# Twenty more small memsets in GpSimd's program, ahead of the constants for the attention sums

## Chip, cores, metric

One core of one Trainium2 chip. The metric is the time of one execution in microseconds (us) on the device; medians of several executions are quoted, and verdicts need 2% to call a kernel faster or slower. A run can fall in a slow state, with a lower granted TensorE clock; such runs are left out of ratios.

## The reference

A layer norm of x (2048 x 512), a sliding, dilated local attention on it (32 heads of 16, a window of 8 keys 2 apart), a gated MLP on it (512 to 1792 to 512), and their combination:

```python
    xn = _layernorm(x, axis=-1)
    s = _A_ref(xn, A_wqkv, A_wo)
    g = _silu(_B_ref(xn, B_w_gate, B_w_up, B_w_down))
    return x + s * g
```

## The kernel before

The kernel works on four groups of 512 positions. GpSimd has little to do: a few constants, and the power -1/2 for the norm of the later tiles. In the code and the views, xn is a normalized tile of x, pk the products of queries and keys, h the gated products of the MLP, pv the products of weights and values; dsum and hsum are constant tiles of zeros and ones by which TensorE sums pk into the attention logits (L_ps) and pv into the outputs (o_ps). The parts that matter here (cuts marked):

```python
    hsum = const.tile([P, H], BF16, name="hsum")
    dsum = const.tile([P, NC, H], BF16, name="dsum")

    def sum_constants():

        nc.gpsimd.memset(dsum[:], 0.0)
        for c in range(NC):
            nc.gpsimd.memset(dsum[:, c, 8 * c : 8 * c + 8], 1.0)
            band(dsum[:, c, 8 * c : 8 * c + 8], 0, 16, 16, 1, 8)   # two affine selects
        for j in range(WL):
            nc.gpsimd.tensor_copy(...)                              # hsum, from ident
    # ...
    def moments(t):
        # ... bn_stats, bn_aggr and + EPS on VectorE
        nc.gpsimd.tensor_tensor(out=rstd[:, t, :], in0=rstd[:, t, :], in1=mhalf[:], op=ALU.pow)
    # ...
    def logits(j):
        # ... TensorE: L_ps, with lhsT=dsum[:, c, :], rhs=the products pk of VectorE
    # ... in the main program, for the first group:
    for t in range(TPQ, 2 * TPQ):
        moments(t)
    sum_constants()
    # ... projections; VectorE: normalize, then pk and h in turn; TensorE: g_ps, u_ps, then logits
```

The softmax here doesn't subtract the row's maximum and nothing guards it: scores larger than these inputs give would overflow.

## Time and profile before

| | |
|---|---|
| time, median of 6 in all | 229.99 us (229.64 to 230.21) |
| span of the profiled execution, first to last instruction | 228.0 us |
| busy share of TensorE / VectorE / ScalarE / GpSimd | 98% / 65% / 57% / 6% |
| GpSimd's constants finished | 21.38 us |
| next GpSimd work, released by VectorE | 32.98 us |
| first read of dsum by TensorE | about 34.05 us |

The first four rows say who limits, the last three where the change goes in: a gap of 11.6 us in a spare engine, with two users behind it. The lines are in the prediction.

### The profile page before, as it was taken

To read this page: it belongs to the slowest core of one execution; us is meant where nothing else is said; L and a number is where in the kernel's file an instruction comes from. 1 tells how busy PE (TensorE), PEld (TensorE's weight loads), DVE (VectorE), ACT (ScalarE), POOL (GpSimd) and SP (SyncE) were. 2 spreads that over 40 slices of the span, in tenths; PEclk is the share of its full clock that TensorE was granted. 3 is DMA by queue.
4 is the path that set the end of the run, shared out by engine and by line. 5 is a ranking of instruction groups with operands and counts; after the bars stand their busy time and mean duration, and the time that the engine had idled before them with its cause. 6 is when DMAs were issued, how large, how long until landed. Compare 5 with 4: busy or idle time off the path is not lost.

```text
span 228.0 us, 3495 instructions
## 1 busy us (share of the span) xinstructions
PE 222.4 (98%) x1300; PEld 106.8 (47%) x1320; DVE 147.6 (65%) x234; ACT 129.8 (57%) x213; POOL 12.8 (6%) x44
## 2 busy tenths in 40 slices
PE   8999999999999999999999999999999999999993
PEld 6864444444444444444444444444444444444453
DVE  4585996999496298865945369735476429943324
ACT  3779769774423876467621686746642387647210
POOL 1046023100000000110000000000000000000000
PEclk9999999999999999999999999999999999999999
DMA  6999589971399211110287511110149700001011
GB/s 166 354 372 372 146 169 197 247 202 38 101 195 206 70 25 29 26 29 0 92 169 168 139 30 23 26 35 5 39 119 206 169 27 3 0 6 26 0 45 48
DMA packets 31264, 24.62 MB, mean 108 GB/s; under 512 B 10896, under 2 KB 31248, under 8 KB 31248
## 3 DMA queue, kind: packets, MB, share of 16 engines
q1 hardware_dynamic: 31248, 24.41, 42.8%
q8 instruction: 10, 0.16, 0.3%
q14 instruction: 6, 0.05, 0.1%
HBM read 18.74 MB, written 4.34 MB: 101 GB/s over the span
## 4 chain that ended last, share of the span: by engine, by line
PE 95%; ACT 2%; issue 1%; DVE 0%; ACTq 0%; DVEq 0%
PE u_ps L238 21%; PE y_ps L394 21%; PE g_ps L238 19%; PE qkv_ps L238 17%; PE s_ps L410 6%; PE L_ps L295 3%; PE o_ps L357 3%; PE warm_ps L220 2%; PE q_ps L238 1%; ACT u L384 1%; ACT L382 1%; PE tr L203 1%; PE den_ps L315 0%; ACT xnT L212 0%; ACT ge L382 0%
## 5 line engine op out<-in xcount | busy, mean ns | idle before, releaser
L238 PE MATMUL u_ps<-xnT,wu_sb 128*128 128x512 bf16 x224 | 57.5, 379 | 0.3
L238 PE MATMUL g_ps<-xnT,wg_sb 128*128 128x512 bf16 x213 | 56.3, 379 | 0.4
L394 PE MATMUL y_ps<-wd_sb,h 128*128 128x512 bf16 (+1 forms) x236 | 50.2, 366 | 0.1
L386 DVE TENSOR_TENSOR h<-ge,u 128x512 bf16<-128x512 bf16 x56 | 23.7, 424 | 37.0 <-ACT u L384 36.6
L284 DVE TENSOR_TENSOR pk<-q_sb,k_sb 128x2048 bf16<-128x2048 bf16 x32 | 37.5, 1216 | 7.0 <-ACT k_sb L259 7.0
L382 ACT ACTIVATE ge<-g_ps 128x512 bf16<-128x512 f32 x56 | 33.5, 598 | 14.9 <-PE g_ps L238 13.8
L384 ACT ACTIVATE u<-u_ps 128x512 bf16<-128x512 f32 x56 | 33.5, 598 | 14.7 <-PE u_ps L238 14.7
L238 PE MATMUL qkv_ps<-xnT,wqkv_sb 128*128 128x512 bf16 (+1 forms) x203 | 40.5, 354 | 0.3
L343 DVE TENSOR_TENSOR pv<-E,v_arr 128x2048 bf16<-128x2048 bf16 x32 | 38.6, 1218 | 0.2 <-issue 0.2
L394 PEld LDWEIGHTS <-h 128*128 128x128 bf16 x238 | 23.3, 98 | 25.3
L238 PEld LDWEIGHTS <-wu_sb 128*128 128x128 bf16 x224 | 21.9, 98 | 26.6 <-issue 0.3
L238 PEld LDWEIGHTS <-wg_sb 128*128 128x128 bf16 x224 | 21.3, 98 | 27.3 <-issue 3.0
L402 ACT ACTIVATE sl<-y_ps 128x512 bf16<-128x512 f32 (+1 forms) x17 | 9.7, 572 | 41.4 <-PE y_ps L394 39.0
L238 PEld LDWEIGHTS <-wqkv_sb 128*128 128x128 bf16 x224 | 21.8, 98 | 19.8 <-issue 0.4
L418 DVE TENSOR_TENSOR m<-s_ps,sl 128x512 bf16<-128x512 f32 (+1 forms) x17 | 11.2, 657 | 22.2 <-PE s_ps L410 22.2
L410 PE MATMUL s_ps<-wo_sb,oT 128*128 128x512 bf16 (+1 forms) x66 | 15.8, 366 | 0.2
L262 ACT ACTIVATE vst<-qkv_ps 128x512 bf16<-128x512 f32 x16 | 9.6, 598 | 6.5 <-PE qkv_ps L238 6.5
L188 POOL TENSOR_TENSOR rstd<-rstd,mhalf 128x1 f32<-128x1 f32 x12 | 7.7, 640 | 87.4 <-DVE rstd L185 87.4
L259 ACT ACTIVATE k_sb<-qkv_ps 128x512 bf16<-128x512 f32 (+1 forms) x20 | 10.2, 516 | 3.5 <-PE qkv_ps L238 3.2
L369 DVE TENSOR_TENSOR oT<-o_ps,rb 128x1024 bf16<-128x1024 f32 x8 | 9.4, 1216 | 3.1 <-DMA rb<-rs_d 3.1
L256 ACT ACTIVATE q_sb<-qkv_ps 128x512 bf16<-128x512 f32 (+1 forms) x16 | 8.7, 544 | 3.2 <-PE qkv_ps L238 3.0
L410 PEld LDWEIGHTS <-oT 128*128 128x128 bf16 x68 | 6.7, 98 | 7.2
(46 smaller groups left out, 105.9 us busy)
## 6 DMA issues: line engine op xcount, KB each, us to landing
v_arr<-vT SPq DMA_DIRECT2D x16, 520.0 KB, 5.4
vT<-vst SPq DMA_DIRECT2D x16, 128.0 KB, 1.8
out_dram<-o_t SPq DMA_DIRECT2D x15, 128.0 KB, 1.8
wg_sb<-in_B_w_gate_dram SPq DMA_DIRECT2D x2, 896.0 KB, 10.7
wu_sb<-in_B_w_up_dram SPq DMA_DIRECT2D x2, 896.0 KB, 12.3
wd_sb<-in_B_w_down_dram SPq DMA_DIRECT2D x1, 1792.0 KB, 12.3
wqkv_sb<-in_A_wqkv_dram SPq DMA_DIRECT2D x3, 512.0 KB, 5.2
x_sb<-in_A_x_dram SPq DMA_DIRECT2D x3, 512.0 KB, 11.6
```

The lines of the kernel that those rows point to most:

```text
L238: nc.tensor.matmul(ps, lhsT=w[:, dk, lo : lo + P], rhs=xnT[j][:, dk, i0 : i0 + n], start=(dk == 0), stop=(dk == NC - 1),)
L259: nc.scalar.activation(out=k_sb[:, c, lo : lo + n], in_=ps, func=AF.Copy)
L262: nc.scalar.activation(out=vst[:], in_=ps, func=AF.Copy)
L284: nc.vector.tensor_tensor(out=pk[:], in0=st[j]["q"][:], in1=k_sb[:, :, off : off + TQ], op=ALU.mult)
L343: nc.vector.tensor_tensor(out=pv[:], in0=st[j]["E"][:, wh, :].unsqueeze(1).to_broadcast([P, 4, TQ]), in1=st[j]["va"][:, 4 * g : 4 * g + 4, ...
L382: nc.scalar.activation(out=ge[:], in_=g_ps[:], func=AF.Gelu_apprx_tanh)
L384: nc.scalar.activation(out=u[:], in_=u_ps[:], func=AF.Copy)
L386: nc.vector.tensor_tensor(out=h[:], in0=ge[:], in1=u[:], op=ALU.mult)
L394: nc.tensor.matmul(y[:], lhsT=st[j][fc][:, tt * P : (tt + 1) * P], rhs=wd_sb[:, fc, cols], start=(fc == 0), stop=(fc == NF - 1),)
L402: nc.scalar.activation(out=sl[:], in_=y[:], func=AF.Silu)
L410: nc.tensor.matmul(s[:], lhsT=st[j]["oT"][:, g, tt * P : (tt + 1) * P], rhs=wo_sb[:, g, cols], start=(g == 0), stop=(g == NC - 1),)
L418: nc.vector.tensor_tensor(out=m[:], in0=s[:], in1=sl[:], op=ALU.mult)
```

## The change

No gain is intended by the memsets themselves: they write a tile that nobody reads, and so ask what work costs that is added to an engine with time to spare.

```diff
+    filler = const.tile([P, 1], F32, name="filler")
+
     def sum_constants():
 
+        for _ in range(20):
+            nc.gpsimd.memset(filler[:], 0.0)
+
         nc.gpsimd.memset(dsum[:], 0.0)
```

## The prediction

> **What bounds the kernel now.** I read four views of the profile, from the whole to the place that the change touches: the page (busy shares and the chain that ended last), the list of who waited for whom, GpSimd's timeline from 16 to 22 us, and the timelines of TensorE and VectorE around the first use of what GpSimd makes there. On the page:
>
> ```profile
> PE 222.4 (98%) x1300; PEld 106.8 (47%) x1320; DVE 147.6 (65%) x234; ACT 129.8 (57%) x213; POOL 12.8 (6%) x44
> ...
> PEclk9999999999999999999999999999999999999999
> ...
> PE 95%; ACT 2%; issue 1%; DVE 0%; ACTq 0%; DVEq 0%
> ```
>
> TensorE is busy for 222.4 of 228.0 us at a full granted clock, and 95% of the chain that ended last runs over TensorE's own instructions. POOL (GpSimd) is busy for 6% and does not appear in that chain at all. So a microsecond of GpSimd's time counts only if TensorE comes to wait for it, directly or through VectorE or ScalarE. The list of waits says how often anybody waits for GpSimd today, and how long GpSimd itself sits idle:
>
> ```profile
> POOL rstd L188 <- DVE rstd L185: 87.4, 12, 52.0
> ...
> DVE xn L194 <- POOL rstd L188: 0.9, 2, 0.4
> ```
>
> Each line gives us in total, how often, and the longest. The first says that GpSimd idled 87.4 us in total before its twelve small power operations. The second is the only line in which another engine waits for GpSimd: 0.9 us in two pieces, on VectorE. The third view is where the new instructions go, between the power at 16.35 us and the memset of dsum at 16.95 us:
>
> ```profile
> 16.35 0.65 POOL L188 TENSOR_TENSOR rstd<-rstd,mhalf 128x1 f32<-128x1 f32 x1 [0.46 <-DVE rstd L185]
> 16.95 0.20 POOL L145 MEMSET dsum<- 128x128 bf16 x1
> 17.21 0.13 POOL L147 MEMSET dsum<- 128x8 bf16 x1
> 17.41 0.25 POOL L130 TENSOR_SCALAR_AFFINE_SELECT dsum<-dsum 128x8 bf16<-128x8 bf16 x1
> 17.73 1.07 POOL L134 TENSOR_SCALAR_AFFINE_SELECT dsum<-dsum 128x8 bf16<-128x8 bf16 x1
> 18.74 0.10 POOL L147 MEMSET dsum<- 128x8 bf16 x1
> 18.91 0.19 POOL L130 TENSOR_SCALAR_AFFINE_SELECT dsum<-dsum 128x8 bf16<-128x8 bf16 x1
> ...
> 20.45 0.93 POOL L150 COPY hsum<-ident 32x32 bf16<-32x32 bf16 x4
> ...
> 32.98 1.39 POOL L188 TENSOR_TENSOR rstd<-rstd,mhalf 128x1 f32<-128x1 f32 x1 [11.60 <-DVE rstd L185]
> ```
>
> The columns are start and duration in us. GpSimd finishes its constants at 20.45 + 0.93 = 21.38 us and then does nothing until 32.98 us: 11.60 us of idle time, ended by VectorE and not by itself. The fourth view shows who uses the constants first:
>
> ```profile
> 33.09 1.03 PE L238 MATMUL u_ps<-xnT,wu_sb 128*128 128x512 bf16 x4
> 34.05 1.91 PE L295 MATMUL L_ps<-pk,dsum 128*32 128x512 bf16 x32
> ```
>
> dsum is first read by TensorE at about 34.05 us (its weight load), 13.5 us after its last affine select ended (20.31 + 0.19 = 20.50 us). hsum is first read at 51.5 us (the view of the tile hsum: first weight load of line 315), 30 us after its copies ended.
>
> **What the Trainium skill says.** GPSIMD Engine Reference, section 2.1 "Instruction dispatch", describes that completion gates whatever waits on an instruction's semaphore, while the next Pool instruction without such a wait may start before it. This matters, because the program of the changed kernel shows 19 of the 20 memsets waiting on GpSimd's own semaphore: they write the same tile, so each waits for the one before. The trace agrees that such a wait costs. Four unrelated memsets in a row at the start begin at 0.31, 0.34, 0.37 and 0.41 us, so about 0.03 us apart, though each is shown with 0.10 us. Where an affine select waits for the memset ahead of it, it begins 0.17 us after it (18.74 to 18.91).
> SBUF — State Buffer, section "Who interferes with whom": a VectorE instruction with two SBUF inputs contends with a GpSimd instruction that reads SBUF, not with one that only writes it, and a VectorE instruction in a two-port mode contends with GpSimd either way; the one that comes second blocks in full. The trace agrees for the first: the affine select at 17.73 took 1.07 us instead of 0.19, and it lies beside VectorE's product pk from 17.53 to 18.74 us. The new memsets only write. Whether the normalizations beside them (xn, line 194) are in a two-port mode, no view here settles.
> Perfetto Trace Analysis, section "GPSIMD Engine Instruction": time GpSimd instructions by the distance from start to start, not by their shown duration. I do so below.
>
> **The change, part by part.** Nothing is removed. The order of instructions on all other engines is the same as before, line numbers apart, and no other engine waits for the new tile. Its one column per partition might shift later tiles' addresses; nothing in the profile gives that a cost, and I book none.
> Added are 20 memsets of 128x1 f32. The distance of a waiting instruction behind a short memset is 0.17 us (three cases: 18.74 to 18.91, and the same for the columns that start at 19.31 and 19.88). The first starts at about 16.95 us, in the place of the dsum memset. 19 x 0.17 = 3.23 us to the start of the last, and the dsum memset follows without a wait, some 0.1 us later: about 3.3 us in all. If the waits were free, 20 x 0.03 = 0.6 us; if each cost what the affine selects do from start to start (18.91 to 19.18, 0.27 us), 5.4 us. So 3.3 us, 0.6 to 5.4.
> Moved: the dsum memset from 16.95 to about 20.3 us, and the rest of the constants with it. Unhindered they take what they took without the blocked select: 21.38 - 16.95 = 4.43 us less 1.07 - 0.19 = 0.88 us, so 3.55 us, which ends at 23.8 us. But now part of them lies beside other VectorE work. Before, VectorE was idle from 18.74 to 21.48 us, in which most selects ran undisturbed. After 21.48 us it is nearly full with h (0.43 us) and pk (1.22 us) in turn, both with two SBUF inputs. From 20.3 to 21.48 us some four of the dozen reading instructions (8 selects, 4 copies) are done; the other eight or nine may each have to wait for the end of a VectorE instruction. One pair of h and pk takes 1.47 us, so a boundary comes every 0.74 us on the average: at worst 9 x 0.74 = 6.7 us from 21.5, so 28.2 us. I expect 24 to 28 us for the end of the hsum copies.
> Against the deadlines: dsum is needed at 34.05 us, the next power at 32.98 us (same engine, in order), hsum at 51.5 us. The nearest is left a margin of 32.98 - 28.2 = 4.8 us at worst. On the path that sets the end the change therefore costs 0.0 us. The sum is 229.84 + 0.0, and I write 229.85 us.
>
> **The rivals.**
> First, the delay gets through: GpSimd holds back the power at 32.98 or the weights dsum at 34.05. It needs 11.6 us more of GpSimd time, so 0.58 us for each memset; the longest short memset shown has 0.13 us. Should it happen, each further us would delay xn and the logits about one to one, and the time would be 230 to 232 us. I give it 2%.
> Second, contention on the shared port: GpSimd's reads slip between VectorE's instructions and delay those by the time of a read. Twelve by 0.19 us is 2.3 us at the outside, in a stretch (21.5 to 33 us) where VectorE is nearly full. For it: VectorE does a pair in 1.47 us while TensorE takes 1.73 us for the two projections beside it (two groups of 0.86 us in the chain), so only about 0.26 us per pair is spare. Against it: TensorE waits for VectorE there in one place only, the last product pk, which ends at 32.75 + 1.21 = 33.96 us and is read in the second half of the logits, after about 34.05 + 1.91/2 = 35.0 us, so there is 1 us to spare; and the pairs that follow give 0.26 us back each, over six pairs 1.6 us. What is left over is 0 to 0.3 us: 229.8 to 230.1 us. I give a visible effect of this kind 10%, and it stays within 2%.
> Third, the normalizations of 16.19 to 17.61 us, should their mode take the shared port, are held up by memsets, each for one memset. Four by 0.1 us is 0.4 us; the transpose that needs the second of them begins on TensorE at 19.5 us, and it was ready before 17.0 us. So nothing again, 229.85 us.
> A gain has no mechanism other than chance: no wait is taken away.
>
> **Range and chances.** The three runs before span 229.64 to 230.21 us, so 0.6 us of scatter where nothing changes. I take that, 0.2 us more below and 0.3 us more above for the second rival: 229.4 to 230.5 us. Two per cent is 4.6 us. Even if all of the 3.3 us landed on the path it would be 1.4%, and the same; only the 5.4 us case wholly on the path would be slower by over 2%. Faster 0.005, same 0.985, slower 0.01.
>
> **What would show each step right or wrong.** In the changed profile: POOL with 64 instructions in place of 44. The new memsets 0.17 us from start to start, the dsum memset at about 20.3 us (17.6 would mean that the waits are free, 22.4 that they cost as much as a select). Several selects or copies stretched from 0.2 to around 1 us beside h or pk, and the copies ended by 24 to 28 us. The power of about 33 us still released by VectorE and not by GpSimd itself, with an idle gap of 4 to 9 us in place of 11.60. The logits starting at 34.05 us within some 0.1 us, TensorE's busy time at 222.4 us within some 0.3, and no wait of TensorE for dsum. The prediction is wrong if the dsum weight load waits for GpSimd, if the time rises by more than 0.7 us, or if a later stage shows TensorE waiting where it did not.

## The result

The changed kernel took 229.56 us in the median of six (the fast ones 229.39 to 229.68), the kernel before 229.99 us. A ratio here is the mean time of one kernel's fast runs over that of the other's of the same rounds, so not quite the ratio of the medians: 0.9981, 95% interval 0.9967 to 0.9994. That is "same" at 2%, inside the predicted range, and 0.3 us below the predicted number. The prediction stands; two things remain to be asked: whether its reason (the work fits in a gap) is the right one, and where the 0.2% comes from, which was not foreseen.

The changed kernel's page, busy time of the engines:

```profile
PE 223.0 (98%) x1320; PEld 106.0 (47%) x1320; DVE 147.5 (65%) x234; ACT 129.7 (57%) x213; POOL 17.2 (8%) x64
```

GpSimd has 64 instructions for 44 and 4.4 us more busy time. VectorE and ScalarE are as before. TensorE's 0.6 us more are no extra work: this trace holds 1320 matmul records, that of before 1300 of the same 1320.

GpSimd's timeline in the changed kernel (start, duration in us; in brackets the idle time before, and who ended it):

```profile
15.56 0.65 POOL L193 TENSOR_TENSOR rstd<-rstd,mhalf 128x1 f32<-128x1 f32 x1 [0.46 <-DVE rstd L190]
16.16 3.31 POOL L148 MEMSET filler<- 128x1 f32 x20
19.40 0.20 POOL L150 MEMSET dsum<- 128x128 bf16 x1
...
21.84 1.02 POOL L130 TENSOR_SCALAR_AFFINE_SELECT dsum<-dsum 128x8 bf16<-128x8 bf16 x1
...
23.15 2.94 POOL L155 COPY hsum<-ident 32x32 bf16<-32x32 bf16 x4
32.75 1.39 POOL L193 TENSOR_TENSOR rstd<-rstd,mhalf 128x1 f32<-128x1 f32 x1 [6.66 <-DVE rstd L190]
```

The memsets hold GpSimd for 19.40 - 16.16 = 3.24 us, 0.162 us each. The selects and copies now lie beside VectorE's products, and some are stretched (1.02 us for a select, 2.94 for four copies that took 0.93). The constants are finished at 23.15 + 2.94 = 26.09 us, 4.7 us later than before. Still 6.66 us of idle time are left before the next power, and VectorE ends it, as before. TensorE's timeline around the first use:

```profile
32.86 1.03 PE L243 MATMUL u_ps<-xnT,wu_sb 128*128 128x512 bf16 x4
33.82 1.91 PE L300 MATMUL L_ps<-pk,dsum 128*32 128x512 bf16 x32
```

The logits follow the projections as before. They begin 0.23 us earlier (33.82 for 34.05), and the span is 0.2 us shorter (227.8 for 228.0). So the difference is there before dsum is used. TensorE's timeline at the start of the kernel before:

```profile
0.84 4.43 PE L220 MATMUL warm_ps<-const-bfloat16-1.0 128*128 128x256 bf16 x22 [0.84 <-PEq L548]
5.13 0.61 PE L203 MATMUL tr<-ident,xn 128*128 128x128 bf16 x4
...
5.95 0.45 PE L203 MATMUL tr<-ident,xn 128*128 128x128 bf16 x4
...
6.88 1.91 PE L238 MATMUL q_ps<-xnT,wqkv_sb 128*128 128x256 bf16 x16 [0.24 <-ACT xnT L212]
```

The same lines of the changed kernel:

```profile
0.83 4.09 PE L225 MATMUL warm_ps<-const-bfloat16-1.0 128*128 128x256 bf16 x22 [0.83 <-PEq L553]
5.12 0.40 PE L208 MATMUL tr<-ident,xn 128*128 128x128 bf16 x4 [0.19 <-DVE xn L199]
...
5.64 0.40 PE L208 MATMUL tr<-ident,xn 128*128 128x128 bf16 x4
...
6.59 1.92 PE L243 MATMUL q_ps<-xnT,wqkv_sb 128*128 128x256 bf16 x16 [0.32 <-DMA wqkv_sb<-in_A_wqkv_dram]
```

In the changed kernel the 22 warm-up matmuls end after 4.09 us instead of 4.43, and the first four transposes take 0.40 us instead of 0.61. The clock record in the trace puts the full clock at 4.41 us, against 6.08 us in the kernel before (the windows view counts the time ahead of that record as full). The first projection gains only part of this, 6.59 us instead of 6.88: in the changed kernel it waits 0.32 us for the load of its weights. The memsets begin at 16.16 us, so this cannot come from their work.

### The profile page after: what moved, and what is told of

The parts are those of the page before. It is cut to its first block, busy times and chain, and to the rows that moved or that the text cites. A ratio compares the mean times of both kernels' runs of the same rounds, so it can differ in the third digit from the quotient of the medians.

```text
span 227.8 us, 3535 instructions
## 1 busy us (share of the span) xinstructions
PE 223.0 (98%) x1320; PEld 106.0 (47%) x1320; DVE 147.5 (65%) x234; ACT 129.7 (57%) x213; POOL 17.2 (8%) x64
## 4 chain that ended last, share of the span: by engine, by line
PE 94%; DMA 2%; ACT 1%; SPq 1%; DVE 0%; issue 0%; DVEq 0%
PE y_ps L399 21%; PE u_ps L243 21%; PE g_ps L243 21%; PE qkv_ps L243 18%; PE s_ps L415 6%; PE L_ps L300 3%; PE o_ps L362 3%; DMA wqkv_sb<-in_A_wqkv_dram 2%; PE q_ps L243 1%; ACT L387 1%; SPq L85 1%; PE den_ps L320 0%; ACT ge L387 0%; ACT vst L267 0%; PE tr L208 0%; ACT xnT L217 0%
## 5 line engine op out<-in xcount | busy, mean ns | idle before, releaser
L243 PE MATMUL g_ps<-xnT,wg_sb 128*128 128x512 bf16 x224 | 57.6, 379 | 0.0
```

Source lines behind the costliest of these rows:

```text
L243: nc.tensor.matmul(ps, lhsT=w[:, dk, lo : lo + P], rhs=xnT[j][:, dk, i0 : i0 + n], start=(dk == 0), stop=(dk == NC - 1),)
```

## The experiments

The theories. **Slack:** the memsets cost nothing because GpSimd's gap is longer than they and what they push; with more of them there is a knee, and beyond it time rises one to one. **No knee:** GpSimd's work is of no account at all. **Port:** memsets and selects disturb VectorE over the shared port, and the time shows it. For the 0.2%: **start** (chance in when TensorE speeds up and loads land), **tile's place** (the filler shifts the addresses of later tiles), **memsets**, and later **v_arr** (when the load of that tile lands). Kernels named e1 share one chip and the runs of the kernel before, likewise e2, e3 and e4. All gave correct results.

### e1_before_again and e1_after_again: both kernels unchanged

No edit.

> The kernel before, unchanged, as a yardstick of its own scatter. Theory A (the 0.43 us by which the changed kernel came out shorter has nothing to do with the memsets, but with the start, when TensorE leaves its slow state and when the first loads land, before GpSimd reaches the memsets at 16 us): this run's profile shows the first q_ps matmul anywhere from 6.5 to 7.0 us and the whole time follows it; median 229.5 to 230.1. Theory B (the memsets or the tile's place make it faster): 229.9 to 230.1 and q_ps at 6.88 again.

> The changed kernel, unchanged, on the same chip as the first. Theory A: ratio to the kernel before between 0.998 and 1.002, with an interval that may or may not hold 1. Theory B: 0.998 again, 0.9967 to 0.9994. In both the memsets from start to start 0.16 us, GpSimd's constants done at about 26 us, the logits at 33.8 to 34.1 us.

Measured: the kernel before against itself 0.9999 (0.9985 to 1.0012; median 229.83 us); the changed kernel 0.9986 (0.9972 to 1.0000; 229.48 us). Their first projections begin at 6.81 and 6.78 us, nearly equal, and so are the spans, 227.9 and 228.0 us. GpSimd's 20 memsets again take 3.24 us (16.08 to 19.32).

### e1_one_memset: the tile without the work

```diff
-        for _ in range(20):
+        for _ in range(1):
```

> One new memset instead of twenty, so the tile is there and the addresses after it are as in the changed kernel, but not the work. If the tile's place makes the gain, the ratio is 0.998 as with twenty; if the twenty memsets make it, the ratio is 1.000 and the changed kernel beside it 0.998. Theory A: 0.998 to 1.002, not tied to either. GpSimd's constants are done at about 21.5 us after the start of the first new memset at 16.2 to 17 us.

Measured: 0.9994 (0.9981 to 1.0006), 229.75 us. It sits between the two and its interval holds both, so it does not tell the tile's place from chance.

### e1_no_wait: the memsets without waits

```diff
-    filler = const.tile([P, 1], F32, name="filler")
+    filler = const.tile([P, 20], F32, name="filler")
...
-        for _ in range(20):
-            nc.gpsimd.memset(filler[:], 0.0)
+        for i in range(20):
+            nc.gpsimd.memset(filler[:, i : i + 1], 0.0)
```

> Twenty memsets to twenty columns of one tile, so none waits for the one before. My step of the waits says 0.03 us from start to start in place of 0.16, 0.7 us for all twenty in place of 3.3, dsum's memset 0.7 us after the first, and the constants done at 21 to 22 us. If a memset cannot start before the last has finished even without a wait, 0.1 us each and 2 us for all. Time as the kernel before, ratio 0.998 to 1.002. The burst lies wholly beside the four normalizations on VectorE: if they use the shared port, they or some memsets are stretched by 0.1 us or more.

Measured: 1.0002 (0.9985 to 1.0020), 229.99 us, six runs from 229.34 to 230.37. Its timeline of GpSimd:

```profile
16.64 0.72 POOL L148 MEMSET filler<- 128x1 f32 x20
17.30 0.20 POOL L150 MEMSET dsum<- 128x128 bf16 x1
```

and of VectorE:

```profile
15.88 2.09 DVE L199 TENSOR_SCALAR xn<-x_sb,mv,rstd 128x512 bf16<-128x512 bf16 x4
17.88 1.21 DVE L289 TENSOR_TENSOR pk<-q_sb,k_sb 128x2048 bf16<-128x2048 bf16 x1
```

The step of the waits is right: 17.30 - 16.64 = 0.66 us for twenty, 0.033 us each instead of 0.162. So four fifths of what the change costs GpSimd are waits for its own last memset. The second reading was not expected in this size: the four normalizations take 2.09 us instead of 1.37 in the changed kernel, and the longest single one 1.13 us instead of 0.41. It began at 16.52 us and ended at 17.65, 0.72 us late and just after the burst and the dsum memset behind it (16.64 to 17.50) were over. The view of the tile xn gives the least, median and longest time in ns; in the kernel before, with one memset, with twenty without waits, and in the changed kernel:

```profile
L194 DVE TENSOR_SCALAR xn<-x_sb,mv,rstd x16: 394/409/465, 4.7 to 102.9; 128x512 bf16<-128x512 bf16 x16
L199 DVE TENSOR_SCALAR xn<-x_sb,mv,rstd x16: 395/410/502, 4.8 to 102.7; 128x512 bf16<-128x512 bf16 x16
L199 DVE TENSOR_SCALAR xn<-x_sb,mv,rstd x16: 395/410/1128, 4.6 to 103.5; 128x512 bf16<-128x512 bf16 x16
L199 DVE TENSOR_SCALAR xn<-x_sb,mv,rstd x16: 405/410/414, 4.6 to 102.6; 128x512 bf16<-128x512 bf16 x16
```

dsum's memset alone holds it up by about 0.06 us, one memset more by 0.04 us, twenty more by 0.66 us, which is 0.033 us each, their own distance. So GpSimd's memsets do hold up xn, and a burst without gaps does so for nearly its whole length. That the shared port is the means fits, but no run takes the port away. With waits between them it is the other way about: in the changed kernel, where the first three of the twenty lie beside normalizations, none of these takes more than 0.414 us, and a memset is stretched to 0.265 us. None of this reached the logits: they begin at 33.87 us.

This profile is 0.6 us longer than the others all the same (228.6 us), and the loss lies later. Who waited for whom, and TensorE's timeline of the second sums:

```profile
DVE pv L348 <- DMA v_arr<-vT: 1.2, 1, 1.2
```

```profile
51.48 1.68 PE L362 MATMUL o_ps<-pv,hsum 128*32 128x512 bf16 x28
53.77 0.40 PE L362 MATMUL o_ps<-pv,hsum 128*32 128x512 bf16 x4 [0.60 <-DVE pv L348]
```

VectorE waited 1.2 us for the load of v_arr, and its last product then held TensorE for 0.60 us; with the smaller gaps beside it the projection behind the sums comes 0.79 us late. The queue began to issue this load at 29.11 us, against 28.0 (before) and 26.2 us (changed). That gave the v_arr theory, tested as e3 and e4.

### e2: 75, 100 and 200 memsets

```diff
-        for _ in range(20):
+        for _ in range(75):     # and 100, 200
```

> 75 memsets. The slack theory: they start at 16.2 us and take 0.162 us each (3.24 us for twenty in the changed kernel), so the last ends near 28.3 us; the eight selects then wait in turn for VectorE's products, at most 0.74 us each, so dsum is ready at 31 to 34 us, about when TensorE wants it (33.9 us), and the power of the ninth tile comes at 34 to 37 us instead of 32.8. Time 229.5 to 231.0, ratio 1.000 to 1.006. The rival, that only GpSimd's work matters and there is no knee: 55 more memsets than the changed kernel cost nothing here and nothing at 100 and 200 either.

> 100 memsets, the last ends near 32.4 us. Slack theory: beyond the knee. dsum ready at 35 to 38 us, TensorE waits for it in the logits' first weight load by 1 to 4 us and the whole time rises by as much: 230.6 to 234 us. A wait of TensorE for GpSimd's dsum shows. The rival without a knee: 229.8.

> 200 memsets, the last ends near 48.6 us. Slack theory: VectorE runs dry before, so the selects are not held up and take 2.5 us; dsum ready at about 51.2 us, TensorE waits from 33.9 to there, 17.3 us, and the time is 229.7 + 17.3 = 247 us (245 to 249); from 100 to 200 memsets the slope is 0.162 us each or a little less. The rival without a knee: 229.8.

Measured against the kernel before (229.99 us on this chip):

| memsets | median us | ratio, 95% interval | memsets end, last select of dsum ends, us |
|---|---|---|---|
| 75 | 229.80 | 0.9984, 0.9958 to 1.0009 | 27.7, 32.5 |
| 100 | 230.55 | 1.0017, 0.9996 to 1.0038 | 31.8, 35.3 |
| 200 | 245.81 | 1.0697, 1.066 to 1.0734 | 47.4, 50.0 |

With 75, dsum is ready at 32.28 + 0.19 = 32.47 us and the logits begin at 34.39 us, 27.17 us after the first projection, as everywhere: no cost at all. This is so although the whole of GpSimd's gap was used up:

```profile
32.42 1.96 POOL L155 COPY hsum<-ident 32x32 bf16<-32x32 bf16 x4
34.46 0.60 POOL L193 TENSOR_TENSOR rstd<-rstd,mhalf 128x1 f32<-128x1 f32 x1
```

The power has no idle time before it and comes about 1.1 us later than it was due (an estimate: 32.98 us, moved by the later start of 7.22 - 6.88 = 0.34 us). By the program it serves the tiles of the third group, whose projections come much later. The time is in the expected range, the ratio just below it. With 100, TensorE's timeline shows the knee:

```profile
33.83 0.78 PE L300 MATMUL L_ps<-pk,dsum 128*32 128x512 bf16 x8
34.78 0.40 PE L300 MATMUL L_ps<-pk,dsum 128*32 128x512 bf16 x4 [0.17 <-POOL dsum L152]
35.34 1.26 PE L300 MATMUL L_ps<-pk,dsum 128*32 128x512 bf16 x20 [0.17 <-POOL dsum L134]
```

TensorE starts in time on the first quarter of dsum, so not with the wait in the first weight load that was expected, then runs into GpSimd, which is still making the later quarters. The projection behind the logits begins at 36.54 instead of 35.7 us (33.83 + 1.84, the logits' undisturbed length), and from the logits' start to the end of the span it takes 194.97 us instead of 193.95: 1.0 us lost, 0.87 of it here and 0.17 at the second sums (o_ps), whose cause was not followed. The median rose by only 0.56 us and the interval holds 1, so by the times alone this step is unclear; it is the trace that shows it. With 200:

```profile
16.03 31.39 POOL L148 MEMSET filler<- 128x1 f32 x200
...
47.35 0.20 POOL L150 MEMSET dsum<- 128x128 bf16 x1
```

```profile
48.30 4.03 PE L300 MATMUL L_ps<-pk,dsum 128*32 128x512 bf16 x32 [13.84 <-POOL dsum L152]
```

TensorE stands still for 13.84 us for GpSimd's dsum: the logits begin at 48.30 us instead of 7.22 + 27.17 = 34.39. After that they take 4.03 us instead of 1.91, and the projections behind them are slow too, 3.2 us in all (from the logits' start to the end 197.2 us instead of 193.95). The granted clock shows why (window, its length, TensorE's busy time and matmuls, granted clock, DMA):

```profile
38.00:48.00 10.00, 0.00 (x0) 0.50 1.11 278
48.30:52.26 3.96, 3.96 (x32) 0.50 0.02 6
```

TensorE lost half its clock while it stood still, and the record has the half clock from 37.42 to 54.49 us. So 13.9 us of stall and 3.2 us of slow clock, with 0.34 us of a later start, make up the 17.5 us by which this span is longer (245.5 for 228.0). The profiled run is the longest of the four (247.20 us). The median is 15.8 us above the kernel before; the other three show a mean granted clock of 0.969 to 0.971 instead of 0.965, so by estimate (span x (1 - clock) x 2) some 14 to 15 us at half clock instead of 17. That the time fell into the expected 245 to 249 us is in part luck: dsum was ready 1.2 us sooner and the wait 3.4 us shorter than expected, and the loss of clock was not expected.

From 100 to 200 memsets GpSimd has 15.6 us more to do (31.32 against 15.72) and the median rises by 245.81 - 230.55 = 15.3 us. That is nearly one to one beyond the knee, but as a sum of parts: the stall alone grew by 13.0 us (13.9 against 0.87), the rest fits the slow clock. The theory without a knee has fallen.

### e2_reads_20: twenty copies in place of the memsets

```diff
-    filler = const.tile([P, 1], F32, name="filler")
+    filler = const.tile([P, 1], BF16, name="filler")
...
-            nc.gpsimd.memset(filler[:], 0.0)
+            nc.gpsimd.tensor_copy(out=filler[:], in_=ident[:, 0:1])
```

> Twenty copies of one column of ident instead of twenty memsets, each waiting for the one before: they read as well as write. Port theory: a copy behind a copy takes about 0.27 us from start to start as the selects do, and those beside pk (16.7 to 17.9 us) are held up by up to 1.2 us, which the memsets in the changed kernel were not (their distances beside pk stayed near 0.16 us). GpSimd's copies end near 22 to 23 us, the constants at 27 to 31 us. Time as the kernel before all the same, 229.4 to 230.3, as it all ends before 32.8 us.

Measured: 0.9981 (0.9961 to 1.0001), 229.64 us. GpSimd's timeline:

```profile
15.88 8.38 POOL L148 COPY filler<-ident 128x1 bf16<-128x1 bf16 x20
24.19 0.20 POOL L150 MEMSET dsum<- 128x128 bf16 x1
...
30.93 1.15 POOL L155 COPY hsum<-ident 32x32 bf16<-32x32 bf16 x4
32.68 1.39 POOL L193 TENSOR_TENSOR rstd<-rstd,mhalf 128x1 f32<-128x1 f32 x1 [0.60 <-DVE rstd L190]
```

Twenty copies that read hold GpSimd for 8.31 us, more than the 6 to 7 us expected, and push the constants deep into VectorE's products; they end at 32.08 us, and only 0.60 us of the gap is left. The whole time does not move, and VectorE's products are not slower for it: pk 1.22 us and h 0.42 us in this stretch, as before. So on GpSimd's reads against VectorE's products, GpSimd pays, not VectorE. In all the traces there are two small exceptions, each beside a GpSimd read that had begun just before: an h of 0.476 us in e1_no_wait (at 21.30 us, the copy at 21.295) and a pk of 1.243 us with 100 memsets (at 32.52 us, the select at 32.50).

### e3: the last load of x put off

```diff
         load_w(wu_sb, B_w_up, lo, hi)
-        load_x((2 + i) * TPQ, TPQ)
+        if i == 0:
+            load_x(2 * TPQ, TPQ)
...
     def load_late_weights():
+        load_x(3 * TPQ, TPQ)
```

> The kernel before, with its last load of x (the fourth group, not needed before 80 us) put off until the late weights, so that the queue reaches the loads of v_arr sooner. Theory: the spread of a few tenths between runs, and with it the 0.2% of the changed kernel, comes from the moment at which v_arr lands (its issue began at 28.0 us before, 26.2 us in the changed kernel, 29.1 us in the run without waits, where VectorE waited 1.2 us for it and TensorE 0.6 us after that). Then v_arr is issued at 25 to 27 us here, and no run is over 229.9 us; median 229.2 to 229.7, ratio 0.997 to 0.9995. The rival, that the spread comes from the start alone (TensorE's slow state): spread and median as in the kernel before, 229.5 to 230.3.

> The changed kernel with the same load put off. If the memsets do nothing for the time, it is as the other within 0.1% (median 229.2 to 229.7). If the twenty memsets themselves gain 0.2% beside the loads, it is 0.4 us shorter than the other.

Measured, both against the kernel before: with the edit in the kernel before 1.0007 (0.9994 to 1.0020; 229.79 us, runs of 230.26 and 230.58 where none was expected over 229.9), with it in the changed one 1.0004 (0.9992 to 1.0016; 229.94 us). v_arr was issued sooner (26.5 and 24.7 us), and the spread stayed. The v_arr theory as the cause of the spread, and of the 0.2%, has fallen. It also gave no faster version. Here the kernel with the memsets has the higher median of the two, by 0.15 us.

### e4: the burst once more, with and without the late load

No edit against e1_no_wait; and e1_no_wait with the edit of e3.

> The twenty memsets without waits once more. In its first run three of six times were 230.25 to 230.37 and its profile showed VectorE waiting 1.2 us for v_arr. If the burst itself makes v_arr late, some two or three of six are at or above 230.2 again and a wait for v_arr shows. If it was chance in the queue of loads before the burst, most are between 229.4 and 230.0. In both the third normalization is stretched to about 1.1 us again, as the burst keeps VectorE off the port.

> The same with the last load of x put off, so that v_arr is issued at about 25 to 27 us and cannot be late. If the times around 230.3 came from v_arr, none is above 230.1 unless TensorE's first projection starts after 7.0 us in it, no wait for v_arr shows, and the stretch from the logits' start to the end is 193.9 to 194.0 us instead of 194.7. If they came from the burst in another way, they stay.

Measured: 0.9980 (0.9968 to 0.9992; five runs from 229.41 to 229.63 us) and 0.9987 (0.9973 to 1.0001; 229.64 us). The longest normalization is 1.13 us in both, so the hold by the burst is no accident. The long runs of e1_no_wait did not come back: a late v_arr was chance in the queue in that series (in the repeat VectorE waited 0.4 us for it, without effect), and not the burst's doing as far as five runs can say. With the late load no run is above 230.04 us and the stretch from the logits to the end is 193.94 us, as expected. Two of the three long runs of e1_no_wait have no profile, so their cause is open.

### The start, over all profiles

From each profile, in us: the start of the first projection (q_ps), the start of the logits, and the span.

| kernel | q_ps | logits | span | logits - q_ps | span - logits |
|---|---|---|---|---|---|
| before | 6.88 | 34.05 | 228.0 | 27.17 | 193.95 |
| changed | 6.59 | 33.82 | 227.8 | 27.23 | 193.98 |
| e1_before_again | 6.81 | 33.98 | 227.9 | 27.17 | 193.92 |
| e1_after_again | 6.78 | 33.98 | 228.0 | 27.20 | 194.02 |
| e1_one_memset | 6.69 | 33.85 | 227.8 | 27.16 | 193.95 |
| e1_no_wait | 6.69 | 33.87 | 228.6 | 27.18 | 194.73 |
| e2_memsets_75 | 7.22 | 34.39 | 228.4 | 27.17 | 194.01 |
| e2_memsets_100 | 6.67 | 33.83 | 228.8 | 27.16 | 194.97 |
| e2_reads_20 | 6.58 | 33.75 | 227.7 | 27.17 | 193.95 |
| e3_before_late_x | 6.60 | 33.77 | 227.7 | 27.17 | 193.93 |
| e3_after_late_x | 7.12 | 34.29 | 228.2 | 27.17 | 193.91 |
| e4_no_wait_again | 6.68 | 33.85 | 227.8 | 27.17 | 193.95 |
| e4_no_wait_late_x | 6.89 | 34.06 | 228.0 | 27.17 | 193.94 |

The span is given to 0.1 us, so the last column is good to about 0.05 us. The middle is the same in all within 0.07 us, whatever stands in GpSimd's program, and the tail too, except for the two with a wait that the trace names. What differs is the moment of the first projection, 6.58 to 7.22 us, and the span follows it.

Two things set this moment in the traces. One is when TensorE speeds up: the clock records put the full clock at 4.12 to 6.70 us, over these profiles and that of 200 memsets. The six in which it came after 5.8 us begin the projection at 6.81 to 7.22 us. The other eight begin it at 6.58 to 6.78 us however early the clock came, since TensorE then waits for data; in both profiles of the changed kernel it waits 0.32 to 0.33 us for the load of wqkv.

The Trainium skill says of the first ("TensorE: Matmul & The Clock Gate", Part 1, "The HAM clock gate") that the activity window is free-running and does not start over with the kernel, so that the transition varies by ±500 ns. The traces agree with a free-running window: within one trace the changes of the clock lie whole multiples of 3.413 us apart (221.86 us or 65 of them in the kernel before, 30.72 and 17.07 us or 9 and 5 with 200 memsets). They do not agree with the size: the transition varies by 2.58 us here, from 3.3 to 5.9 us after the first matmul at 0.84 us.

## Why the prediction was right

- **GpSimd is spare and the path is TensorE's.** Shown: 75 memsets, 11.8 us, cost nothing, and the stretch from the first projection to the logits is 27.16 to 27.23 us from none to 100.
- **19 x 0.17 + 0.1 = 3.3 us.** Measured 3.24 us, and the waits are its larger part (0.66 us without them). Where nothing lies beside them the memsets are 0.156 us apart, not 0.17; the three beside normalizations are further apart. The moment, dsum's memset at 20.3 us, was 0.9 us off (19.40), because the whole of VectorE's norm work before it came 0.8 us sooner (the power at 15.56 for 16.35); in that view a load of x ends VectorE's idle time.
- **Constants done by 24 to 28 us, an idle gap of 4 to 9 us.** Measured 26.09 and 6.66 us, with the stretched selects and copies that were described.
- **First rival, the delay gets through.** The threshold was mis-sized: "It needs 11.6 us more of GpSimd time" took the power at 32.98 us for a deadline. 75 memsets, 11.8 us, held the power back by about 1.1 us and cost nothing, so a late power did not delay the logits. The deadline that binds is dsum: 15.7 us cost 1.0 us in the trace, 31.3 us cost 15.8 us in the median. The knee lies between 11.8 and 15.7 us. TensorE also needs only a quarter of dsum at its start.
- **Second rival, contention with products.** It did not happen beyond single cases of 0.05 us: pk and h keep 1.22 and 0.42 us beside waiting selects and copies. The sign "TensorE's busy time at 222.4 us within some 0.3" was missed (223.0), but by the records that the trace of before lacks.
- **Third rival, normalizations held by memsets.** Half wrong. Memsets and normalizations do get in each other's way, but "each for one memset" failed: with waits the memsets gave way, and a burst without waits held one normalization up by 0.72 us. Off the path either way.
- **Logits within 0.1 us of 34.05.** Missed by 0.23 us. The step that failed is silent in the prediction: it took the start of the kernel as fixed, where profiles vary by 0.64 us. The 229.85 us were 0.3 us too high for the same reason as far as the profiled pair goes. That the range of 1.1 us still held the result owes to the scatter that it allowed for, not to a reckoning of the start.

What stays open: the ratio of the changed kernel was 0.9981 and 0.9986 in two series, and near it in four of the variants with a filler (0.9980 to 0.9987), but 0.9994 with one memset, and 1.0002 and 1.0004 in two others. In the profiled pair the difference lies before 7 us, ahead of the memsets, and in every profile the stretch behind it is the same but for the named waits, so their work is not the cause there. The runs without a profile cannot be placed; whether a program with the new tile starts a tenth of a per cent sooner on the average, or this is chance, these runs do not settle.

## What to carry to other kernels

Read what added work costs from the gap behind it: when does its engine next have work that others need, and who ends the idle time now. If that gap is longer than the work and all that it pushes, the cost is zero. Its end need not be the knee: 75 memsets filled it for nothing, as the next work in it was not urgent. The knee is where TensorE itself first waits, here for dsum, and beyond it the cost is about one to one, with a surcharge if TensorE stands still so long that it loses its clock (3.2 us here). Before explaining a few tenths of a microsecond, find where in the trace the two runs part: if it is ahead of the first changed instruction, the change did not do it.

## What the Trainium skill lacked or had wrong

- "GPSIMD Engine Reference", section 2.1: it gives no figure for a wait of GpSimd on its own last instruction. Here a 128x1 memset costs 0.156 us from start to start with such a wait (0.162 in the mean of the twenty) and 0.033 us without.
- "SBUF — State Buffer", "Who interferes with whom": it speaks of the port held for one instruction, not of a burst. Here 20 memsets without waits and the one behind them held a VectorE normalization up by 0.72 us (1.13 us instead of 0.41), 0.033 us for each; with 0.156 us between the memsets VectorE was not held and a memset was (0.265 us instead of 0.10).
- The same section says that the order of issue decides who blocks, without a measured pair for a two-input VectorE instruction and a GpSimd read. Here pk and h stayed at 1.22 and 0.42 us, and selects of 0.19 us went up to 1.07 us; where a read had begun just before, an h took 0.476 us and a pk 1.243 us.
- "TensorE: Matmul & The Clock Gate", Part 1, has the spread of the transition too small: it says ±500 ns, and over 14 profiles it came 3.3 to 5.9 us after the first matmul, a range of 2.6 us. After a stall of 13.84 us the full clock came back 6.2 us after the restart, and 32 matmuls took 4.03 us instead of 1.91.
